# A QK-norm attention followed by a low-rank mixer MLP: two passes through DRAM against one fused pass with token rows on chip

## The chip, the cores and the metric

The kernel runs on one core of one Trainium2 chip. The metric is device time in microseconds (us), from the first to the last instruction of one execution as the device counts it; lower is better. The engines have short names in the profile: PE is the matmul engine (TensorE), PEld its weight loads, DVE is VectorE, ACT is ScalarE, POOL is GpSimd, and SP issues most of the DMAs. "L109" is line 109 of the kernel that the line comes from.

## The reference, cut to what matters

```python
# q, k, v: (8, 12, 448, 64) float32, as (batch, head, token, head_dim)
def rmsnorm(x, g):
    return x / np.sqrt(np.mean(x * x, axis=-1, keepdims=True) + 1e-06) * g
q_n, k_n = rmsnorm(q, g_q), rmsnorm(k, g_k)
scores = (1 / np.sqrt(64)) * q_n @ k_n.transpose(0, 1, 3, 2)
attn = softmax(scores)                      # over the last axis
attn_out = attn @ v
x = attn_out.transpose(0, 2, 1, 3).reshape(8, 448, 768)

# U: (448, 32), V: (32, 448), w_ch1: (768, 3072), w_ch2: (3072, 768)
h = (x.transpose(0, 2, 1) @ U @ V).transpose(0, 2, 1)     # mixes tokens, rank 32
u = x + h
out = u + np.maximum(u @ w_ch1, 0.0) @ w_ch2
```

(`softmax` stands for six lines of the reference that subtract the maximum, exponentiate and divide by the sum.)

## The kernel before

It has two stages. Attention works with the head dimension on partitions, so its result is transposed and every head's denominator is a single row on one partition. It goes to DRAM. The MLP stage first loads and casts all weights, builds the full mixing matrix `I + U V`, and then reads the attention result back.

```python
# attention, for each of 8 x 12 heads
for ki in range(NSP):                                     # NSP = 4
    sc = psum.tile([SP, S], FP32, tag="sc")               # SP = 112, S = 448
    nc.tensor.matmul(sc, knT[:, ki * SP:(ki + 1) * SP], qnT, start=True, stop=True)     # L106
    sce = work.tile([SP, S], BF16, tag="sce")
    nc.scalar.activation(sce, sc, AF.Exp, scale=scal)
    nc.tensor.matmul(avT, va_all[:, ki, h, :], sce, ...)                                # L109
den = work.tile([1, S], FP32, tag="den")
nc.vector.reciprocal(den, avT[D:D + 1, :])                                              # L111
denb = work.tile([D, S], FP32, tag="denb")
nc.gpsimd.partition_broadcast(denb, den)
oT = work.tile([D, S], BF16, tag="oT")
nc.vector.tensor_mul(oT, avT[:D, :], denb)
nc.sync.dma_start(x_scratch[b, h * D:(h + 1) * D, :], oT)
# ... cut: the norm of q and k per batch, the transposes of each head (L97)

# MLP, for each of 8 batches, after all weights are loaded and cast
# ... cut: load xT, transpose to xb, uTb = mixing with the 448 x 448 matrix (L176)
for hti in range(KH):                                     # KH = 24, KD = 6
    for dti in range(KD):
        nc.tensor.matmul(ph1, w1b[:, dti, hti * P:(hti + 1) * P], uTb[:, dti, :], ...)  # L184
    nc.scalar.activation(hT[:, hti, :], ph1, AF.Relu)
for dti in range(KD):
    for hti in range(KH):
        nc.tensor.matmul(po, w2b[:, hti, dti * P:(dti + 1) * P], hT[:, hti, :], ...)    # L192
    nc.vector.tensor_add(ofin, po, uTb[:, dti, :])
    # ... cut: transpose back to token rows, copy to osb
```

The softmax here doesn't subtract the row's maximum and nothing guards it: scores larger than these inputs give would overflow.

Of the kernel before, what the change touches and what calls it, by code (L numbers as in the profile page):

```python
# [9 lines left out]
FP32 = mybir.dt.float32  # L11
BF16 = mybir.dt.bfloat16
AX = mybir.AxisListType.X
AF = mybir.ActivationFunctionType


@with_exitstack
def kernel(
# [21 lines left out]
    SP = 112  # L40
    NSP = S // SP
    assert S == SP * NSP
    KD = dm // P
    KH = dh // P

    import dataclasses as _dc
    dram = ctx.enter_context(tc.tile_pool(name="dram", bufs=1, space=bass.MemoryType.DRAM))
    x_scratch = dram.tile([B, dm, S], BF16)
    KS = NSP

    with tc.tile_pool(name="a_const", bufs=1) as consts, \
         tc.tile_pool(name="a_norm", bufs=2) as npool, \
         tc.tile_pool(name="a_work", bufs=3) as work, \
         tc.tile_pool(name="a_ps", bufs=2, space=bass.MemoryType.PSUM) as psum, \
         tc.tile_pool(name="a_ps2", bufs=2, space=bass.MemoryType.PSUM) as psum2, \
         tc.tile_pool(name="a_ps3", bufs=2, space=bass.MemoryType.PSUM) as psum3:

        ident = consts.tile([P, P], BF16)
        make_identity(nc, ident)
        scal = 1.0 / (D ** 0.5)  # L60

        g_qs = consts.tile([D, 1], FP32)
        nc.sync.dma_start(g_qs, g_q.rearrange("(d o) -> d o", o=1))
        g_ks = consts.tile([D, 1], FP32)
        nc.sync.dma_start(g_ks, g_k.rearrange("(d o) -> d o", o=1))

        def rmsnorm_b(src, tag):
            t = npool.tile([SP, NSP, H, D], FP32, tag=tag + "_t")
            for so in range(NSP):
                nc.sync.dma_start(t[:, so, :, :], src[so * SP:(so + 1) * SP, :, :])  # L70
            sq = npool.tile([SP, NSP, H, D], FP32, tag=tag + "_sq")
            nc.scalar.activation(sq, t, AF.Square)  # L72
            ssq = npool.tile([SP, NSP, H], FP32, tag=tag + "_ssq")
            nc.vector.tensor_reduce(ssq, sq, AX, AluOpType.add)  # L74
            nc.scalar.activation(ssq, ssq, AF.Copy, scale=1.0 / D, bias=1e-6)
            nc.vector.reciprocal(ssq, ssq)
            nc.scalar.sqrt(ssq, ssq)  # L77
            ob = npool.tile([SP, NSP, H, D], BF16, tag=tag + "_ob")
            nc.vector.tensor_tensor(ob, t, ssq.rearrange("p a h -> p a h ()").to_broadcast([SP, NSP, H, D]), AluOpType.mult)  # L79
            return ob  # L80

        for b in range(B):
            qnb = rmsnorm_b(q.rearrange("b h s d -> b s h d")[b], "q")
            knb = rmsnorm_b(k.rearrange("b h s d -> b s h d")[b], "k")
            vt = npool.tile([SP, NSP, H, D], FP32, tag="vt")
            for so in range(NSP):
                nc.sync.dma_start(vt[:, so, :, :], v.rearrange("b h s d -> b s h d")[b, so * SP:(so + 1) * SP, :, :])
            va_all = npool.tile([SP, NSP, H, D + 1], BF16, tag="vaall")
            nc.gpsimd.memset(va_all[:, :, :, D:D + 1], 1.0)
            nc.vector.tensor_copy(va_all[:, :, :, :D], vt)  # L90

            for h in range(H):
                qkT = []
                for (src, gs, tg) in [(qnb, g_qs, "qT"), (knb, g_ks, "kT")]:
                    pt = psum2.tile([D, S], BF16, tag="pt")
                    for si in range(NSP):
                        nc.tensor.transpose(pt[:, si * SP:(si + 1) * SP], src[:, si, h, :], ident[:SP, :SP])  # L97
                    tT = work.tile([D, S], BF16, tag=tg)
                    nc.scalar.activation(tT, pt, AF.Copy, scale=gs)  # L99
                    qkT.append(tT)  # L100
                qnT, knT = qkT

                avT = psum3.tile([D + 1, S], FP32, tag="avT")
                for ki in range(NSP):
                    sc = psum.tile([SP, S], FP32, tag="sc")
                    nc.tensor.matmul(sc, knT[:, ki * SP:(ki + 1) * SP], qnT, start=True, stop=True)  # L106
                    sce = work.tile([SP, S], BF16, tag="sce")
                    nc.scalar.activation(sce, sc, AF.Exp, scale=scal)  # L108
                    nc.tensor.matmul(avT, va_all[:, ki, h, :], sce, start=(ki == 0), stop=(ki == NSP - 1))  # L109
                den = work.tile([1, S], FP32, tag="den")  # L110
                nc.vector.reciprocal(den, avT[D:D + 1, :])  # L111
                denb = work.tile([D, S], FP32, tag="denb")
                nc.gpsimd.partition_broadcast(denb, den)  # L113
                oT = work.tile([D, S], BF16, tag="oT")
                nc.vector.tensor_mul(oT, avT[:D, :], denb)  # L115
                nc.sync.dma_start(x_scratch[b, h * D:(h + 1) * D, :], oT)

    with tc.tile_pool(name="m_const", bufs=1) as mconsts, \
         tc.tile_pool(name="m_work", bufs=2) as work, \
         tc.tile_pool(name="m_ps", bufs=2, space=bass.MemoryType.PSUM) as psum, \  # L120
         tc.tile_pool(name="m_psout", bufs=2, space=bass.MemoryType.PSUM) as psum_out:

        identmb = mconsts.tile([P, P], BF16)
        make_identity(nc, identmb)
        w1b = mconsts.tile([P, KD, dh], BF16)
        w2b = mconsts.tile([P, KH, dm], BF16)
        Wb = mconsts.tile([SP, KS, S], BF16)
        with tc.tile_pool(name="m_tmp", bufs=1) as tmp:
            for i in range(KD):
                wf = tmp.tile([P, dh], FP32, tag="wf")  # L130
                nc.sync.dma_start(wf, moe_w_ch1.rearrange("(o i) h -> i o h", i=P)[:, i, :])
                nc.vector.tensor_copy(w1b[:, i, :], wf)  # L132
            for i in range(KH):
                wf = tmp.tile([P, dm], FP32, tag="wf")
                nc.sync.dma_start(wf, moe_w_ch2.rearrange("(o i) d -> i o d", i=P)[:, i, :])
                nc.vector.tensor_copy(w2b[:, i, :], wf)  # L136

            ident2 = tmp.tile([P, P], FP32, tag="ident2")
            make_identity(nc, ident2)
            Ub = tmp.tile([rank, S], BF16, tag="uvb")  # L140
            for si in range(KS):
                Us = tmp.tile([SP, rank], FP32, tag="us")
                nc.sync.dma_start(Us, moe_U[si * SP:(si + 1) * SP, :])
                Upt = psum.tile([rank, SP], FP32, tag="ps1")
                nc.tensor.transpose(Upt, Us, ident2[:SP, :SP])
                nc.vector.tensor_copy(Ub[:, si * SP:(si + 1) * SP], Upt)
            Vb = tmp.tile([rank, S], BF16, tag="uvb2")
            Vf = tmp.tile([rank, S], FP32, tag="uvf")
            nc.sync.dma_start(Vf, moe_V)
            nc.vector.tensor_copy(Vb, Vf)  # L150
            idstripe = tmp.tile([SP, S], FP32, tag="ids")
            for si in range(KS):
                pw = psum.tile([SP, S], FP32, tag="ps1")
                nc.tensor.matmul(pw, Ub[:, si * SP:(si + 1) * SP], Vb, start=True, stop=True)
                nc.gpsimd.memset(idstripe, 0.0)
                nc.gpsimd.affine_select(out=idstripe, in_=idstripe,
                                        compare_op=AluOpType.not_equal, fill=1.0,
                                        base=si * SP, pattern=[[-1, S]], channel_multiplier=1)
                nc.vector.tensor_add(pw, pw, idstripe)
                nc.vector.tensor_copy(Wb[:, si, :], pw)  # L160

        for b in range(B):
            xT = work.tile([P, KD, S], BF16, tag="xT")
            nc.sync.dma_start(xT, x_scratch.rearrange("b (do di) s -> b di do s", di=P)[b])
            xb = work.tile([SP, KS, dm], BF16, tag="xb")
            for dti in range(KD):
                xpt = psum.tile([SP, KS, P], BF16, tag="psx")
                for si in range(KS):
                    nc.tensor.transpose(xpt[:, si, :], xT[:, dti, si * SP:(si + 1) * SP], identmb)
                nc.vector.tensor_copy(xb[:, :, dti * P:(dti + 1) * P], xpt)  # L170

            uTb = work.tile([P, KD, S], BF16, tag="uTb")
            for dti in range(KD):
                ph = psum.tile([P, S], FP32, tag="ps1")
# [57 lines left out]
```

## Time and profile before

The time is 1167.03 us, the median of two runs (1166.46 to 1167.61). The profiled execution spans 1165.7 us.

| what | before |
|---|---|
| attention, start to last value matmul | 0 to 579 us |
| first MLP matmul (L184) | 618 us |
| PE busy | 1004.5 us, 86% |
| DVE busy | 601.6 us, of which the reciprocals 281.9 us |
| same 448 columns, distance of back-to-back matmul starts | 379 ns in attention, 189 ns in the MLP |

The first line below is the page's list of busy times, the others are from its rows of 40 slices, in which a digit is the busy share in tenths and PEclk is the clock granted to the matmul engine.

```profile
PE 1004.5 (86%) x4424; PEld 457.6 (39%) x4424; DVE 601.6 (52%) x483; ACT 495.7 (43%) x847; POOL 94.3 (8%) x122
...
PE   0888788788988899999744996999999999999997
DVE  3688989998788769667754121330212212130302
PEclk9999999999999999999996898899999999999998
```

PE looks busy nearly everywhere. The dent in slices 20 to 22 is the wait for weights between the stages. DVE is near its limit in the first half and little used in the second.

The next lines are the page's groups: line, engine, operation, output and input, shape and count, then total busy us and the mean ns of one, and after the second bar the idle time before it and what ended that.

```profile
L111 DVE RECIPROCAL den<-avT 1x448 f32<-1x448 f32 x96 | 281.9, 2944 | 80.3 <-PE avT L109 79.1
...
L109 PE MATMUL avT<-sce,va_all 112*65 112x448 bf16 x384 | 196.1, 571 | 46.4 <-ACT sce L108 43.8
L106 PE MATMUL sc<-tT 64*112 64x448 bf16 x384 | 217.1, 599 | 14.2 <-ACT sce L108 13.1
```

One reciprocal of 448 numbers on one partition takes 2.944 us. The reciprocals do not bound the stage alone: over the 579 us of attention PE is busy for 478.3 us and DVE for 460.1 us, DVE more in the first half and PE more in the second. The windows below give busy us of each engine in a stretch, then the granted clock, the DMA share and GB/s.

```profile
480.00:540.00 60.00, 57.52 (x181) 21.95 (x179) 39.86 (x23) 36.02 (x68) 8.26 (x12) 1.00 0.05 12
573.00:660.00 87.00, 48.40 (x217) 24.01 (x218) 37.81 (x55) 10.56 (x20) 7.15 (x15) 0.86 0.51 176
840.00:900.00 60.00, 60.00 (x330) 30.89 (x329) 10.40 (x17) 13.06 (x24) 0.00 (x0) 1.00 0.07 24
```

In the same 60 us PE executes 181 matmuls of attention and 330 of the MLP, and is about fully busy in both. The timeline explains that. Its columns are start, duration of the run of instructions, engine, line, operation and count.

```profile
501.77 1.81 PE L109 MATMUL avT<-sce,va_all 112*65 112x448 bf16 x4
503.51 0.62 PE L106 MATMUL sc<-tT 64*112 64x448 bf16 x1
...
859.70 1.30 PE L184 MATMUL ph_6161<-uTb,w1b 128*128 128x448 bf16 x6
```

Four matmuls of 448 columns take 1.81 us in attention, and six of 448 columns take 1.30 us in the MLP. From the start times in the trace the distances are 379 and 189 ns. The array runs attention at half clock, although the PEclk row shows nines there. The recorded clock has no change before 616.6 us, and the profile takes that for full speed.

### The profile page before, as it was taken

To read this page: it belongs to the slowest core of one execution; us is meant where nothing else is said; L and a number is where in the kernel's file an instruction comes from. 1 tells how busy PE (TensorE), PEld (TensorE's weight loads), DVE (VectorE), ACT (ScalarE), POOL (GpSimd) and SP (SyncE) were. 2 spreads that over 40 slices of the span, in tenths; PEclk is the share of its full clock that TensorE was granted. 3 is DMA by queue.
4 is the path that set the end of the run, shared out by engine and by line. 5 is a ranking of instruction groups with operands and counts; after the bars stand their busy time and mean duration, and the time that the engine had idled before them with its cause. 6 is when DMAs were issued, how large, how long until landed. Compare 5 with 4: busy or idle time off the path is not lost.

```text
span 1165.7 us, 11492 instructions
## 1 busy us (share of the span) xinstructions
PE 1004.5 (86%) x4424; PEld 457.6 (39%) x4424; DVE 601.6 (52%) x483; ACT 495.7 (43%) x847; POOL 94.3 (8%) x122
## 2 busy tenths in 40 slices
PE   0888788788988899999744996999999999999997
PEld 0333233333333333333221443455555555555553
DVE  3688989998788769667754121330212212130302
ACT  3677877777676665666400421004040312112130
POOL 0012312211111111111110000000000000000000
PEclk9999999999999999999996898899999999999998
DMA  9567766243260000000075334011010202010101
GB/s 179 96 105 129 127 117 117 53 96 58 45 120 8 13 10 12 13 12 8 12 260 191 109 109 127 18 42 41 1 48 1 71 1 71 1 48 1 48 1 48
DMA packets 153703, 74.79 MB, mean 64 GB/s; under 512 B 133904, under 2 KB 146224, under 8 KB 152880
## 3 DMA queue, kind: packets, MB, share of 16 engines
q1 hardware_dynamic: 153648, 74.06, 27.7%
q8 instruction: 34, 0.56, 0.2%
q14 instruction: 21, 0.17, 0.0%
HBM read 57.52 MB, written 16.52 MB: 64 GB/s over the span
## 4 chain that ended last, share of the span: by engine, by line
PE 69%; ACT 9%; DMA 8%; issue 7%; DVE 5%; POOL 1%; SPq 0%; POOLq 0%; ACTq 0%; DVEq 0%
PE po L192 18%; PE sc L106 13%; PE avT L109 13%; DMA wf<-in_moe_w_ch_dram 7%; PE pt L97 6%; ACT sce L108 4%; PE ph L176 3%; ACT tT L99 2%; PE ot L198 2%; DVE w2b L136 1%; ACT L77 1%; ACT L108 1%; DVE ob L79 1%; DVE den L111 1%; DVE w1b L132 1%
## 5 line engine op out<-in xcount | busy, mean ns | idle before, releaser
L111 DVE RECIPROCAL den<-avT 1x448 f32<-1x448 f32 x96 | 281.9, 2944 | 80.3 <-PE avT L109 79.1
L108 ACT ACTIVATE sce<-sc 112x448 bf16<-112x448 f32 x384 | 200.0, 542 | 158.3 <-PE sc L106 115.3
L192 PE MATMUL po<-hT,w2b 128*128 128x448 bf16 x1152 | 231.5, 356 | 13.1 <-DVE w2b L136 12.9
L109 PE MATMUL avT<-sce,va_all 112*65 112x448 bf16 x384 | 196.1, 571 | 46.4 <-ACT sce L108 43.8
L106 PE MATMUL sc<-tT 64*112 64x448 bf16 x384 | 217.1, 599 | 14.2 <-ACT sce L108 13.1
L195 DVE TENSOR_TENSOR ofin<-po,uTb 128x448 bf16<-128x448 f32 x48 | 29.9, 625 | 312.2 <-PE po L192 312.2
L184 PEld LDWEIGHTS <-w1b 128*128 128x128 bf16 x1152 | 113.3, 99 | 125.6 <-DVE w1b L132 17.5
L192 PEld LDWEIGHTS <-w2b 128*128 128x128 bf16 x1152 | 110.3, 98 | 115.7 <-DVE w2b L136 19.9
L97 PE MATMUL pt<-ident,ob 112*64 112x112 bf16 x768 | 103.4, 292 | 40.1 <-DVE ob L79 31.4
L106 PEld LDWEIGHTS <-tT 64*112 64x112 bf16 x384 | 61.2, 178 | 168.1 <-issue 160.0
L113 POOL PARTITION_BROADCAST denb<-den x96 | 86.4, 900 | 461.6 <-DVE den L111 461.5
L97 PEld LDWEIGHTS <-ob 112*64 112x64 bf16 x768 | 74.3, 159 | 121.2 <-PE sc L106 42.5
L109 PEld LDWEIGHTS <-va_all 112*65 112x65 bf16 x384 | 51.3, 146 | 102.4 <-issue 85.1
L115 DVE TENSOR_TENSOR oT<-avT,denb 64x448 bf16<-64x448 f32 x96 | 59.2, 617 | 18.2 <-POOL denb L113 16.8
L99 ACT ACTIVATE tT<-pt,g_ks 64x448 bf16<-64x448 bf16 x96 | 59.7, 622 | 8.0 <-PE pt L97 4.3
L74 DVE TENSOR_REDUCE ssq<-sq 112x48 f32<-112x3072 f32 x16 | 53.0, 3311 | 19.1 <-ACT sq L72 19.1
L99 ACT ACTIVATE tT<-pt,g_qs 64x448 bf16<-64x448 bf16 x96 | 59.5, 620 | 3.0 <-PE pt L97 1.9
L79 DVE TENSOR_TENSOR ob<-t,ssq 112x3072 bf16<-112x3072 f32 x16 | 53.2, 3325 | 1.4 <-ACT ssq L77 1.4
L136 DVE CAST w2b<-wf 128x768 bf16<-128x768 f32 x24 | 13.4, 560 | 65.6 <-DMA wf<-in_moe_w_ch_dram 65.6
L176 PE MATMUL ph<-Wb,xb 112*128 112x448 bf16 x192 | 44.2, 368 | 1.2 <-DVE uTb L178 0.6
L72 ACT ACTIVATE sq<-t 112x3072 f32<-112x3072 f32 x16 | 44.1, 2754 | 0.0
L199 DVE CAST osb<-ot 112x512 f32<-112x512 bf16 x48 | 33.1, 690 | 21.1 <-PE ot L198 21.1
(420 smaller groups left out, 599.4 us busy)
## 6 DMA issues: line engine op xcount, KB each, us to landing
t<-in_q_dram SPq DMA_DIRECT2D x32, 336.0 KB, 5.1
t<-in_k_dram SPq DMA_DIRECT2D x32, 336.0 KB, 5.3
vt<-in_v_dram SPq DMA_DIRECT2D x32, 336.0 KB, 5.8
out_dram<-osb SPq DMA_DIRECT2D x32, 336.0 KB, 4.2
wf<-in_moe_w_ch_dram SPq DMA_DIRECT2D x6, 1536.0 KB, 6.7
wf<-in_moe_w_ch_dram SPq DMA_DIRECT2D x24, 384.0 KB, 3.0
x_scratch<-oT SPq DMA_DIRECT2D x96, 56.0 KB, 1.9
xT<-x_scratch SPq DMA_DIRECT2D x8, 672.0 KB, 4.8
```

The lines of the kernel that those rows point to most:

```text
L79: nc.vector.tensor_tensor(ob, t, ssq.rearrange("p a h -> p a h ()").to_broadcast([SP, NSP, H, D]), AluOpType.mult)
L97: nc.tensor.transpose(pt[:, si * SP:(si + 1) * SP], src[:, si, h, :], ident[:SP, :SP])
L99: nc.scalar.activation(tT, pt, AF.Copy, scale=gs)
L106: nc.tensor.matmul(sc, knT[:, ki * SP:(ki + 1) * SP], qnT, start=True, stop=True)
L108: nc.scalar.activation(sce, sc, AF.Exp, scale=scal)
L109: nc.tensor.matmul(avT, va_all[:, ki, h, :], sce, start=(ki == 0), stop=(ki == NSP - 1))
L111: nc.vector.reciprocal(den, avT[D:D + 1, :])
L113: nc.gpsimd.partition_broadcast(denb, den)
L115: nc.vector.tensor_mul(oT, avT[:D, :], denb)
L176: nc.tensor.matmul(ph, xb[:, si, dti * P:(dti + 1) * P], Wb[:, si, :], start=(si == 0), stop=(si == KS - 1))
L184: nc.tensor.matmul(ph1, w1b[:, dti, hti * P:(hti + 1) * P], uTb[:, dti, :], start=(dti == 0), stop=(dti == KD - 1))
L192: nc.tensor.matmul(po, w2b[:, hti, dti * P:(dti + 1) * P], hT[:, hti, :], start=(hti == 0), stop=(hti == KH - 1))
```

## The change

The intent is one pass. A token of a batch is taken as `4 p + j`, so that one DMA row holds four tokens. The value product is turned around, so that the exponentials are the stationary operand and tokens land on partitions. Denominators then sit one to a partition, and the division is a small reciprocal of 128 x 4 and a multiply. Attention output stays in SBUF. Mixing is two small products of rank 32. The second MLP product makes `hT` stationary, so token rows come out and need no transpose. Weights are cast by their DMA. The squares and the inverse root of the norm move to POOL. The instructions of the next batch's attention are written ahead of this batch's MLP, and a scheduler interleaves them in each engine's fixed order. The core of the diff, with cuts:

```diff
-            nc.scalar.activation(sq, t, AF.Square)
-            nc.vector.tensor_reduce(ssq, sq, AX, AluOpType.add)
-            nc.scalar.activation(ssq, ssq, AF.Copy, scale=1.0 / D, bias=1e-6)
-            nc.vector.reciprocal(ssq, ssq)
-            nc.scalar.sqrt(ssq, ssq)
+            for s in range(2):
+                nc.gpsimd.tensor_tensor(sq[:, s], qk[:, s], qk[:, s], OP.mult)           # L150
+            nc.vector.tensor_reduce(rstd..., sq..., AX, OP.add)                          # L152
+            nc.gpsimd.tensor_scalar(rstd, rstd, D * 1e-6, None, OP.add)                  # L154
+            nc.gpsimd.tensor_tensor(rs, rs, mhalf, OP.pow)                               # L156
...
+                    nc.vector.tensor_tensor(qkn..., qk..., rstd..., OP.mult)             # L163
...
-                    nc.tensor.matmul(avT, va_all[:, ki, h, :], sce, ...)
-                nc.vector.reciprocal(den, avT[D:D + 1, :])
-                nc.gpsimd.partition_broadcast(denb, den)
-                nc.vector.tensor_mul(oT, avT[:D, :], denb)
-                nc.sync.dma_start(x_scratch[b, h * D:(h + 1) * D, :], oT)
+                    o = ps_o.tile([P, 4, D + 1], FP32, tag="o")            # one buffer
+                    for i, off in enumerate(OFFS[par]):
+                        for kc in range(NJ):
+                            nc.tensor.matmul(o[:, i, :], E[:, hh, c:c + P], va[:, hl, kc, :], ...)  # L193
+                    nc.vector.reciprocal(rec, o[:, :, D])                                # L196
+                    nc.vector.tensor_tensor(x3[:, :, d0:d0 + D], o..., rec..., OP.mult)  # L197
+                    nc.vector.tensor_tensor(xs[rows, d0:d0 + D], o..., rec..., OP.mult)  # L200
...
-                for hti in range(KH):
-                    nc.tensor.matmul(po, w2b[:, hti, dti * P:(dti + 1) * P], hT[:, hti, :], ...)
-                for si in range(KS):
-                    nc.tensor.transpose(ot[:, si, :], ofin[:, si * SP:(si + 1) * SP], identmb)
+                for hc in range(KH):
+                    nc.tensor.matmul(po, hT[:, hc, i * P:(i + 1) * P], w2b[:, hc, hs], ...)  # L270
...
+    attention(0)
+    load_weights(state["gate"])
+    setup_mix()
+    mix(0)
+    attention(1)
+    mlp(0)
+    for b in range(1, B):
+        mix(b)                                   # L217 to L236
+        if b + 1 < B:
+            attention(b + 1)
+        mlp(b)                                   # w1: L250, w2: L270
```

## The prediction

> **What bounds the kernel now.** The 1165.7 us span has two stages that hardly overlap. Until about 575 us it is attention. There, by the busy-time windows, PE is 48 to 57 busy of 60 us, DVE 40 to 56. The MLP runs from 600 us; from 780 us PE is 60 of 60. Between them, 573 to 660 us and again 713 to 735 us, PE waits for weights (the chain of waits: issue 18.4 us, `wf` loads 4 to 7 us each).
>
> The distance between matmul starts tells more than busy time. In the MLP, 448 columns start 189 ns apart. In attention, back-to-back `avT` matmuls of the same 448 columns start 379 ns apart, `sc` 415 ns, transposes 93 ns against 48 to 56. The clock row shows full speed there; I distrust it: attention runs at half clock. The Trainium skill, "TensorE: Matmul & The Clock Gate", Part 1, says low activity halves the clock; the trace agrees by spacing. Attention's matmuls fill under half of the array (64x112, 112x65). The recorded drops at 623 and 719 us follow about 30% array use; 66% kept full clock.
>
> **Removed.** The 2.94 us reciprocals on one partition (282 us of DVE), the broadcasts, the DRAM round trip, 30 table loads (38 us of ACT), both transposes around the MLP, the weight bubble (about 100 us).
>
> **PE after, per batch, warm (estimates from the spacings).** MLP columns are unchanged: w1 144 at 189 = 27.2 us, w2 168 at about 163 = 27.3, V products 1.3. Transposes 48 at 50 = 2.4. Scores 48 in row halves, 5 to 10. Values: 192 pairs of a 128-column load and 65 moving columns, 30 to 60 ns each, 6 to 11. Mixing 3.5. Sum 73 to 83 us, over eight batches 585 to 665.
>
> **DVE after, per batch**, at about 1.04 ns per element plus 150 ns: reduce 6.7, qkn 8.0, q/k copies 4.7, per-head normalisation 9.3, mixing 5.3, relus 7.5, adds 3.9 = 45 us. ACT: 24 exps of 896 columns at about 0.92 us, plus relus = 28. POOL about 25, with `pow` unmeasured.
>
> **Critical path.** The instruction order gives, per batch, an attention stretch (next batch's attention with about half of w1) and a dense tail (other half of w1, then w2; 41 us). The stretch holds about 37 us of PE and 38 us of DVE; with one `o` bank, one `t` bank and a fixed order I expect 42 to 50 us. So 86 us a batch. Startup, attention 0 alone (cold) and attention 1 beside mlp 0, with 19 MB of weights arriving: mlp 0 ends near 150 us. Then 6 x 86 + 63 (last batch, no attention) gives about **735 us**, range 665 to 860. Faster by over 2%: 0.97; within 2%: 0.02; slower: 0.01.
>
> **Right if:** 384-column `po` start about 163 ns apart; w1 matmuls inside the attention stretch keep 163 to 216 ns (warm); DVE about 360 us in total, no reciprocal group above 25 us; PE has no gap above 10 us after about 130 us; the tail is about 41 us, the stretch 42 to 50.
>
> **Wrong if:** the stretch falls back to half clock: w1 there at about 375 ns, +30 us a batch, 900 us. Or POOL's `pow`, or its descriptor writing for the casting weight loads, takes many microseconds and starves attention at the start; or the fixed order stalls PE on DVE's chain after each head.

## The result and the profile after

The time is 857.29 us, the median of two runs (855.32 to 859.25). Ratios here are the mean time of one kernel's fast runs over that of the other's of the same rounds, so not quite the ratio of the quoted medians: 0.734, with a 95% interval of 0.7318 to 0.7363. The time fell by 310 us where 432 were predicted. It is inside the range that was given, but at its upper edge (860). All outputs are right.

First the page of the profile after, its busy times and its row of slices:

```profile
PE 688.1 (80%) x5168; PEld 383.7 (45%) x5168; DVE 373.7 (44%) x749; ACT 215.4 (25%) x289; POOL 274.9 (32%) x162
...
PE   0365576898679976798679976799868998998997
POOL 5885676301760016700661005630275000000000
PEclk9995587799899996899989999789969999999999
```

DVE fell to 373.7 us, near the 360 predicted. PE is no longer full: it dips once in each batch, and the granted clock dips with it. POOL works in bursts at the same places. Where POOL has no more bursts, from slice 32 on, the dips are gone.

The groups show the terms that were costed and one that was not:

```profile
L270 PE MATMUL po<-w2b,hT 128*128 128x384 bf16 x1344 | 227.5, 326 | 0.0
L150 POOL TENSOR_TENSOR sq<-qk 112x1024 f32<-112x1024 f32 x48 | 95.9, 2011 | 289.8 <-DMA qk<-in_q_dram 288.3
...
L156 POOL TENSOR_TENSOR rstd<-rstd,mhalf 112x32 f32<-112x32 f32 x24 | 131.1, 5460 | 1.7
L163 DVE TENSOR_TENSOR qkn<-qk,rstd 112x512 bf16<-112x512 f32 x96 | 98.0, 1041 | 54.5 <-POOL rstd L156 54.1
```

The `pow` takes 5.46 us for 32 numbers on each partition, 24 times. That is 131.1 us of POOL's 274.9. The multiply that waits for it, `qkn`, takes 1041 ns in the mean, where 0.665 us was assumed (8.0 us a batch, twelve of them).

The list of waits says who stands behind whom: the engine and line that waited, what it waited for, total us, times, longest us.

```profile
DVE qkn L163 <- POOL rstd L156: 54.1, 10, 13.9
...
DVE rstd L152 <- POOL sq L150: 39.2, 12, 6.4
PE o L193 <- DVE xs_103 L200: 38.2, 12, 7.3
PE o L193 <- DVE xs_104 L200: 32.6, 13, 5.4
```

DVE waits for POOL, and PE's value product waits for DVE to empty the one `o` buffer. Three timelines of the same ten microseconds show how one leads to the other (a bracket gives the idle time before and what ended it). First DVE's:

```profile
326.84 0.17 DVE L196 RECIPROCAL rec<-o 128x4 f32<-128x4 f32 x1
331.13 2.37 DVE L163 TENSOR_TENSOR qkn<-qk,rstd 112x512 bf16<-112x512 f32 x1 [4.12 <-POOL rstd L156]
333.43 0.34 DVE L197 TENSOR_TENSOR x_2592<-o,rec 128x192 bf16<-128x192 f32 x1
333.79 0.23 DVE L200 TENSOR_TENSOR xs_104<-o,rec 64x64 bf16<-64x64 f32 x1
```

POOL's timeline over the same time:

```profile
325.64 5.46 POOL L156 TENSOR_TENSOR rstd<-rstd,mhalf 112x32 f32<-112x32 f32 x1
331.07 1.89 POOL L150 TENSOR_TENSOR sq<-qk 112x1024 f32<-112x1024 f32 x1
```

And PE's:

```profile
329.30 0.62 PE L182 MATMUL sc<-qT,kT 64*112 64x448 bf16 x1
334.16 1.04 PE L193 MATMUL o<-va_101,E_98 112*128 112x65 bf16 x16 [4.25 <-DVE xs_104 L200]
```

The reciprocal at 326.84 belongs to the attention that is being computed, and the two normalising multiplies (L197, L200) needed only its result. But the first `qkn` of the batch after that one stands between them in DVE's order, and it waits for the `pow`. So DVE is idle for 4.12 us with ready work behind the wait. PE stands at the value product of the next head for 4.25 us, with ready w1 matmuls behind it.

The `qkn` at 331.13 also took 2.37 us, and it ran beside POOL's squares. The longest of all took 4.14 us (61.91 to 66.05), while POOL squared from 61.44 to 65.51; the median is 0.68 us. The Trainium skill, "SBUF — State Buffer", section "Who interferes with whom", states that a DVE instruction with two SBUF inputs contends with a GpSimd instruction that reads SBUF, and that the later one blocks. The times agree: all 30 `qkn` of more than 0.8 us started while POOL was busy, and 28 of them ended 0.54 to 0.56 us after the end of the square or the cast of v that POOL was running at their start.

The windows below are three whole batches, from the start of one mixing to that of the next:

```profile
502.40:597.10 94.70, 76.76 (x625) 45.13 (x625) 46.31 (x95) 25.83 (x36) 32.80 (x15) 0.91 0.22 57
597.10:704.40 107.30, 93.74 (x674) 49.32 (x674) 45.80 (x91) 27.43 (x36) 32.35 (x15) 0.92 0.18 45
704.40:780.90 76.50, 71.02 (x621) 43.12 (x620) 33.27 (x88) 25.78 (x36) 0.00 (x0) 1.00 0.06 17
```

The third holds a whole attention too, that of the last batch, but no norm for a batch after it. It executes about as many matmuls as the first, at full clock, and is 18.2 us shorter. So the scheduler puts the norm of batch b+2 into the attention of batch b+1, and the batch pays for it.

With the start times of the trace, each batch splits at its last value matmul. Up to there is what the prediction called the stretch, and the rest is its tail:

| mixing starts at us | stretch | tail | sum |
|---|---|---|---|
| 192.8 | 58.0 | 48.5 | 106.5 |
| 299.3 | 61.5 | 33.9 | 95.4 |
| 394.7 | 59.2 | 48.5 | 107.7 |
| 502.4 | 60.7 | 34.0 | 94.7 |
| 597.1 | 58.8 | 48.5 | 107.3 |
| mean of five | 59.6 | 42.7 | 102.3 |
| 704.4 (no norm inside) | 36.4 | 40.1 | 76.5 |
| predicted | 42 to 50 | 41 | 86 |

(Tails alternate because a batch's w2 covers three or four tiles of tokens.)

### The profile page after: what moved, and what is told of

Same layout as the page of the kernel before. It is cut to its first block, busy times and chain, and to the rows that moved or that the text cites. A ratio compares the mean times of both kernels' runs of the same rounds, so it can differ in the third digit from the quotient of the medians.

```text
span 857.2 us, 12102 instructions
## 1 busy us (share of the span) xinstructions
PE 688.1 (80%) x5168; PEld 383.7 (45%) x5168; DVE 373.7 (44%) x749; ACT 215.4 (25%) x289; POOL 274.9 (32%) x162
## 4 chain that ended last, share of the span: by engine, by line
PE 53%; DVE 22%; POOL 18%; DMA 4%; issue 2%; ACT 1%; ACTq 0%; SPq 0%; POOLq 0%
PE po L270 25%; PE ph L250 19%; POOL rstd L156 10%; DVE qkn L163 8%; DVE rstd L152 6%; POOL sq L150 6%; PE o L193 3%; DMA qk<-in_q_dram 2%; DVE uB L236 2%; PE pu L227 2%; DVE uA L233 1%; PE sc L182 1%; PE pu L230 1%; DMA vt<-in_v_dram 1%; DVE qT L175 1%
## 5 line engine op out<-in xcount | busy, mean ns | idle before, releaser
L270 PE MATMUL po<-w2b,hT 128*128 128x384 bf16 x1344 | 227.5, 326 | 0.0
L150 POOL TENSOR_TENSOR sq<-qk 112x1024 f32<-112x1024 f32 x48 | 95.9, 2011 | 289.8 <-DMA qk<-in_q_dram 288.3
L270 PEld LDWEIGHTS <-hT 128*128 128x128 bf16 x1344 | 131.5, 98 | 86.9
L253 ACT ACTIVATE hT<-ph 128x384 bf16<-128x384 f32 (+1 forms) x96 | 52.3, 545 | 460.3 <-PE ph L250 460.1
L250 PE MATMUL ph<-uB,w1b 128*128 128x512 bf16 x576 | 146.5, 396 | 2.2 <-ACT hT L253 1.9
L250 PE MATMUL ph<-uA,w1b 128*128 128x384 bf16 x576 | 126.8, 357 | 16.2 <-DVE uA L233 14.3
L156 POOL TENSOR_TENSOR rstd<-rstd,mhalf 112x32 f32<-112x32 f32 x24 | 131.1, 5460 | 1.7
L163 DVE TENSOR_TENSOR qkn<-qk,rstd 112x512 bf16<-112x512 f32 x96 | 98.0, 1041 | 54.5 <-POOL rstd L156 54.1
L184 ACT ACTIVATE E_99<-sc 112x896 bf16<-112x896 f32 x96 | 83.4, 917 | 57.9 <-PE sc L182 43.1
L184 ACT ACTIVATE E_98<-sc 112x896 bf16<-112x896 f32 x96 | 83.2, 917 | 57.0 <-PE sc L182 31.6
L182 PE MATMUL sc<-qT,kT 64*112 64x448 bf16 x384 | 83.2, 433 | 8.7 <-DVE kT L176 3.3
L193 PEld LDWEIGHTS <-E_98 112*128 112x128 bf16 x768 | 36.5, 110 | 83.5 <-issue 42.7
L171 PEld LDWEIGHTS <-qkn 112*128 112x128 bf16 x384 | 23.4, 105 | 60.2 <-DVE qkn L163 43.9
L193 PEld LDWEIGHTS <-E_99 112*128 112x128 bf16 x768 | 33.8, 107 | 20.2 <-issue 10.2
L193 PE MATMUL o<-va_102,E_98 112*128 112x65 bf16 x256 | 13.7, 216 | 29.7 <-DVE xs_103 L200 16.4
L196 DVE RECIPROCAL rec<-o 128x4 f32<-128x4 f32 x96 | 17.1, 178 | 40.1 <-PE o L193 39.9
```

The costliest lines, as they stand in the source:

```text
L150: nc.gpsimd.tensor_tensor(sq[:, s], qk[:, s], qk[:, s], OP.mult)
L156: nc.gpsimd.tensor_tensor(rs, rs, mhalf, OP.pow)
L163: nc.vector.tensor_tensor(qkn[:, s].rearrange("p j h d -> p h j d"), qk[:, s, hp].rearrange("p h (j d) -> p h j d", d=D), rstd[:, s, hp].r ...
L171: nc.tensor.transpose(pt[:, s, j * SP:(j + 1) * SP], qkn[:, s, j].rearrange("p h d -> p (h d)"), ident[:SP, :SP])
L182: nc.tensor.matmul(sc[:, hh, 0:S], kT[pp, kc * SP:(kc + 1) * SP], qT[pp, :], start=True, stop=True)
L184: nc.scalar.activation(E[:, :, PAD + kc * S:PAD + (kc + 1) * S], sc[:, :, 0:S], AF.Exp, scale=float(D) ** 0.5)
```

## The experiments

Theory A: the norm on POOL is what holds the stretch, through DVE's and PE's fixed orders. Theory B: q and k come too late, because two load buffers are too few (POOL's squares waited 288.3 us for them in the list of waits). Theory C: one `o` and one `t` bank hold the stretch whatever the norm costs. Every ratio is to the kernel before, whose median in the three jobs was 1164.83, 1164.35 and 1166.05 us.

| run | what it is | us (runs) | ratio |
|---|---|---|---|
| after | the change | 857.29 (2) | 0.734 |
| e1_rsqrt_dve | inverse root on DVE | 787.97 (4) | 0.6763 |
| e2_loads3 | third load buffer | 856.77 (4) | 0.7352 |
| e3_sq_act | squares on ACT | 781.29 (4) | 0.6704 |
| e5_pow2 | `pow` twice | 948.81 (4) | 0.8163 |
| e4_rsqrt_sq | e1 and e3 | 749.26 (4) | 0.6426 |
| e7_o2t2 | two `o`, two `t` banks | 836.32 (4) | 0.7185 |
| e10_rsqrt_sq_o2t2 | e4 and e7 | 744.45 (4) | 0.6396 |
| e9_rsqrt_sq_pu | e4, mixing product in the MLP's banks | 721.04 (4) | 0.6179 |
| e13_rsqrt_sq_pu_s3o2 | e9 with other score banks | 743.56 (4) | 0.6364 |
| e8_barrier | the change, stages kept apart | 1085.76 (4) | 0.9327 |
| e11_rsqrt_sq_barrier | e4, stages kept apart | 916.05 (4) | 0.7851 |
| e12_before_warm | before, with dummy matmuls | 1276.07 (2) | 1.0928 |

### The inverse root on DVE, the squares on ACT, and the `pow` doubled

e1 takes `add` and `pow` from POOL and computes the inverse root on DVE, from a shifted start value and two Newton steps. It leaves out the epsilon; the output still matched.

```diff
-            nc.gpsimd.tensor_scalar(rstd, rstd, D * 1e-6, None, OP.add)
-            nc.gpsimd.tensor_tensor(rs, rs, mhalf, OP.pow)
+            nc.vector.tensor_scalar(t.bitcast(I32), rs.bitcast(I32), 1, None, OP.logical_shift_right)
+            nc.vector.tensor_scalar(y.bitcast(I32), t.bitcast(I32), -1, 0x5f3759df, OP.mult, OP.add)
+            for it in range(2):
+                nc.vector.scalar_tensor_tensor(t, y, -0.5, y, OP.mult, OP.mult)
+                nc.vector.tensor_tensor(t, t, rs, OP.mult)
+                nc.vector.scalar_tensor_tensor(rs if it else y, t, 1.5, y, OP.add, OP.mult)
```

> Edit: the POOL add and pow (5.46 us each) are replaced by eight small DVE operations (bit-shift seed and two Newton steps) that directly follow the reduce on the same queue. Theory A (the in-order DVE queue holds the next batch's qkn, which waits for pow, ahead of this batch's per-head work, and PE waits for that through the one o bank): qkn waits on POOL rstd (54 us) vanish, part of the reduce waits (39 us) and of the half-clock time with them; about 785 us, 760 to 815. Rival B (the loads are late because only two load buffers exist, so POOL starts late, and the length of pow is secondary): within 2% of 857. Rival C (one o bank and one t bank stall PE whatever the norm does): within 2% of 857.

Measured: 787.97 us (785.83 to 789.81), against an expected 785. (Of the two POOL operations taken away, the `pow` is the one of 5.46 us; the `add` took 0.30 us.) The eight new instructions cost DVE 52.9 us in all, and yet the kernel is 69 us faster. B and C both fall as the main cause, for neither lets this edit gain anything.

e3 leaves `pow` where it is and moves the squares to ACT (1071 ns each there).

```diff
-                nc.gpsimd.tensor_tensor(sq[:, s], qk[:, s], qk[:, s], OP.mult)
+                nc.scalar.activation(sq[:, s], qk[:, s], AF.Square)
```

> Edit: the squares go from POOL (2.0 us each) to ACT as Square activations; pow stays on POOL. Theory A plus [...]contention (qkn takes 0.68 us alone and up to 4.1 us while POOL squares): qkn mean falls from 1.04 to about 0.70 us, the chain before each reduce is 2 us shorter, about 820 us (795 to 845). Rival B and C: within 2% of 857.

Measured: 781.29 us, 76 us less than the change, which is more than was expected. The list of waits of e3:

```profile
DVE qkn L163 <- POOL rstd L156: 37.1, 10, 5.7
...
PE o L193 <- DVE xs L200: 30.6, 13, 6.8
```

DVE's wait for the `pow` fell from 54.1 to 37.1 us, and the wait of PE's value product from 70.8 to 30.6 us. `qkn` fell from 1041 to 717 ns in the mean, 98 to 66.7 us in all: with no squares on POOL, little is left to block it. Theory A alone had left that part out. The edit also makes the squares themselves shorter (1.07 us on ACT, 2.01 us on POOL) and frees POOL of them; which of these parts brings how much of the 76 us was not separated.

e5 computes the `pow` a second time, into a tile that nobody reads, before the real one.

```diff
+            rs2 = norm.tile([SP, 2 * HG * NJ], FP32, tag="rs2")
+            nc.gpsimd.tensor_tensor(rs2, rs, mhalf, OP.pow)
             nc.gpsimd.tensor_tensor(rs, rs, mhalf, OP.pow)
```

> Edit: every pow is done twice on POOL, the first into a spare tile; results unchanged. If pow sits on the critical chain (theory A) most of the 24 extra pows of 5.46 us (131 us) show: 930 to 985 us. If it is hidden (B, C): less than 20 us more, 857 to 877.

Measured: 948.81 us (947.74 to 958.62), 91.5 us more. The added work is another 131 us of POOL, so 70% of it shows in the time. In the list of waits of e5 PE's value product now waits more than twice as long:

```profile
PE o L195 <- DVE xs L202: 153.1, 26, 11.1
DVE rstd L152 <- POOL sq L150: 103.5, 15, 15.8
...
DVE qkn L165 <- POOL rstd L158: 77.4, 12, 9.7
```

POOL, busy for only 32% of the change's span, is thus on the critical path.

### Both at once

e4 holds the edits of e1 and of e3 together.

> Edit: both earlier edits together, reciprocal root on DVE and squares on ACT; POOL keeps only the v cast and the weight loads. Theory A: the two shorten one chain at different places (pow 5.5 us; squares 4 us and the slowed qkn), so the savings of 69 and 76 us should mostly add: 735 us, 710 to 760, DVE waits for the norm (qkn on POOL rstd, reduce on sq) under 20 us in sum, half clock after the first full-clock stretch under 50 us. If both only removed the same wait: 770 to 785.

Measured: 749.26 us (742.3 to 752.75), against an expected 735. Windows of e4, for the batches from 407.6 to 664.3 us:

```profile
407.60:492.00 84.40, 76.73 (x625) 44.58 (x625) 46.41 (x119) 31.09 (x42) 3.67 (x3) 0.92 0.24 64
492.00:587.80 95.80, 87.33 (x667) 47.71 (x676) 46.53 (x115) 32.52 (x42) 3.24 (x3) 1.00 0.20 51
587.80:664.30 76.50, 71.05 (x625) 43.10 (x625) 33.22 (x88) 25.74 (x36) 0.00 (x0) 1.00 0.06 17
```

With POOL out of the norm, the five steady batches take 93.8, 80.0, 94.5, 84.4 and 95.8 us, 89.7 in the mean. Their stretches, by the start times in the trace, are 41.1, 43.9, 40.9, 48.2 and 46.2 us, where the prediction had 42 to 50. mlp 0 ends at 139 us instead of 193. No start-to-start gap of PE after 130 us is longer than 1.6 us, where the change had gaps up to 7.6. In e4's list of waits PE's value product waits for DVE for 7.2 us, where the change had 70.8. The page's chain of the work that ended last, by engine, says the same. In the change it is:

```profile
PE 53%; DVE 22%; POOL 18%; DMA 4%; issue 2%; ACT 1%; ACTq 0%; SPq 0%; POOLq 0%
```

And in e4, where POOL is no longer in it:

```profile
PE 61%; DVE 19%; DMA 10%; ACT 6%; issue 3%; ACTq 0%; SPq 0%
```

### More load buffers

```diff
-    opool = ctx.enter_context(tc.tile_pool(name="opool", bufs=3))
+    opool = ctx.enter_context(tc.tile_pool(name="opool", bufs=2))
-            qk = loads.tile([SP, 2, HG, NJ * D], FP32, tag="qk")
+            qk = loads.tile([SP, 2, HG, NJ * D], FP32, tag="qk", bufs=3)
-            rstd = norm.tile([SP, 2, HG, NJ], FP32, tag="rstd")
+            rstd = norm.tile([SP, 2, HG, NJ], FP32, tag="rstd", bufs=3)
```

> Edit: three qk buffers and three rstd buffers in place of two, paid for with two osb buffers in place of three; pow stays on POOL. Theory A: helps only where pow thereby moves into the dense tail; 820 us, 790 to 850. Rival B: POOL works in the tail, the stretch falls from 71-75 us to near the 52 us of the last one; about 765 us. Rival C: within 2% of 857.

Measured: 856.77 us (853.11 to 859.4), no difference. POOL's squares still wait 283.0 us for `qk`. Loads are released by the `qkn` of an earlier group, inside the stretch, and a third buffer only shifts that by one group. So this miss is of the edit: it does not test loads that arrive early in the tail, and that question stays open. It does show that more buffers alone buy nothing in the sum: the five steady batches take 98.6 us in the mean instead of 102.3, but mlp 0 ends at 205 us instead of 193. The run also narrows theory A. In these five batches DVE's `qkn` no longer waited for the `pow` (20.7 us in the change), but its reduce waited 46.9 us for POOL's squares instead of 28.1. So it is POOL's whole chain of the norm that holds the stretch, not only the wait at the `pow`.

### More banks

```diff
-    ps_s = ctx.enter_context(tc.tile_pool(name="ps_s", bufs=2, space=bass.MemoryType.PSUM))
-    ps_o = ctx.enter_context(tc.tile_pool(name="ps_o", bufs=1, space=bass.MemoryType.PSUM))
-    ps_t = ctx.enter_context(tc.tile_pool(name="ps_t", bufs=1, space=bass.MemoryType.PSUM))
+    ps_s = ctx.enter_context(tc.tile_pool(name="ps_s", bufs=1, space=bass.MemoryType.PSUM))
+    ps_o = ctx.enter_context(tc.tile_pool(name="ps_o", bufs=2, space=bass.MemoryType.PSUM))
+    ps_t = ctx.enter_context(tc.tile_pool(name="ps_t", bufs=2, space=bass.MemoryType.PSUM))
```

> Edit: PSUM only, of the changed kernel: two o banks and two t banks, paid for with one score tile of two banks in place of two. Rival C (the single o and t banks hold PE): 857 falls by over 5%, to about 800. Theory A (PE waits for DVE, which waits for the norm; another o bank only delays that by one head, and one score tile exposes exp): 840 to 890.

Measured: 836.32 us, 2.4% faster than the change, and just under what theory A gave (840 to 890). C has a small part. The same edit on e4:

> Edit: reciprocal root on DVE and squares on ACT, plus the two o and two t banks with one score tile. Once DVE no longer waits for the norm, what is left of PE's waits is for the o and t banks: if those count, 20 to 40 us under e4_rsqrt_sq; if the single score tile costs as much (PE then waits for exp, 0.92 us, before each score pair), within 10 us of it or slower.

Measured: 744.45 us against 749.26, no clear difference, since e4's own runs spread from 742.3 to 752.75. The steady batches got shorter (91.2, 76.3, 90.5, 75.6 and 90.2 us), but the start got longer: mlp 0 ends at 172 us instead of 139. With the single score tile PE's score products waited 34.6 us for exponentials in the first 170 us, where e4 has 9.1 us of that wait in its whole span. So the banks are needed in more than one place. Moving one tile to a pool that has room at that moment does better:

```diff
-            pu = ps_t.tile([P, S], FP32, tag="t")
+            pu = ps_mm.tile([P, S], FP32, tag="mm")
```

> Edit: e4_rsqrt_sq with the mixing product pu in the two mm banks in place of the single t bank. In the mixing PE waits 0.65 us for each of six evacuations per batch; two banks should hide most of it: 720 to 742 us. If the w1 filler that used the mm banks there is only pushed back: within 1% of 749.

Measured: 721.04 us (720.2 to 723.61), the best version of all. It is 0.6179 of the time before, and 136 us under the change. Its row of slices:

```profile
PE   0685699999899999999899998998999999999997
PEclk9996899999999999999999999999999999999999
```

The dips are gone; what is left is the start. Stretches are now 39.9, 39.6, 38.6, 39.1 and 38.3 us. In the last try, three score banks of one head each and two `o` banks were put on top:

```diff
-    ps_s = ctx.enter_context(tc.tile_pool(name="ps_s", bufs=2, space=bass.MemoryType.PSUM))
-    ps_o = ctx.enter_context(tc.tile_pool(name="ps_o", bufs=1, space=bass.MemoryType.PSUM))
+    ps_s = ctx.enter_context(tc.tile_pool(name="ps_s", bufs=3, space=bass.MemoryType.PSUM))
+    ps_o = ctx.enter_context(tc.tile_pool(name="ps_o", bufs=2, space=bass.MemoryType.PSUM))
-                    sc = ps_s.tile([SP, 2, 512], FP32, tag="s")
+                    scs = [ps_s.tile([SP, 512], FP32, tag="s", name=f"sc{hh}") for hh in range(2)]
```

(The matmuls and the exponentials follow: one of each per head.)

> Edit: e9_rsqrt_sq_pu with one score bank per head (three of them) in place of two pairs, exp of 448 columns in place of 896, and two o banks from the bank set free. PE no longer waits for xs between heads: 700 to 735 us. If the doubled number of exps (26 in place of 22 us a batch) or the score banks hold PE instead: 740 or more.

Measured: 743.56 us, slower than e9. The edit also doubled the number of exponentials, and which of its parts costs the 22 us was not separated.

### What the overlap is worth

Barriers of all engines keep mixing, attention and MLP apart; nothing else differs from the change.

```diff
         mix(b)
         if b + 1 < B:
+            tc.strict_bb_all_engine_barrier()
             attention(b + 1)
+            tc.strict_bb_all_engine_barrier()
         mlp(b)
```

(A third barrier stands between `attention(1)` and `mlp(0)`.)

> Edit: the changed kernel with an all-engine barrier before and after each attention from the second on, so that attention and MLP of one batch no longer overlap; all instructions stay. If the overlap carries a part of the gain: mixing 10, attention 45 to 55, MLP 62 us in turn, 960 to 1060 us, attention at half clock again (w1 not in it). If the gain comes from removed work alone: 840 to 900.

Measured: 1085.76 us, above the 960 to 1060 expected, 229 us more than the change and 7% under before. The same barriers on e4:

> Edit: e4_rsqrt_sq with the barriers of e8_barrier. It asks how much of the 229 us that the barriers cost was overlap of attention with the MLP and how much was the norm chain laid bare. If overlap (and the clock that w1 keeps up): still over 150 us slower than e4_rsqrt_sq, 900 to 960. If it was mostly the norm chain: under 850.

Measured: 916.05 us, 167 us more than e4. So with the norm off POOL, the removed work and shorter stages alone take before's time down by 250 us, and interleaving takes another 167. That is not PE's overlap alone: the barriers also hold back the loads and the norm of the next batch, and PE's transposes wait 93.4 us for `qkn` in e11, against 16.1 in e4. In the change interleaving also hid part of the POOL chain, which is the likely reason for the difference of 62 us between the two figures (229 and 167). A part of both figures is the clock: after the first return to full clock, the trace's clock records add up to 476 us at half clock in e8 and 322 in e11, against 151 in the change and 41 in e4.

### The clock in the kernel before

If attention ran at half clock because it uses too little of the array, added dummy matmuls should raise the clock and bring the known full-clock distances.

```diff
                     nc.tensor.matmul(avT, va_all[:, ki, h, :], sce, ...)
+                    for _ in range(4):
+                        nc.tensor.matmul(dum, wdum[:SP, :], sce, start=True, stop=True)
```

> Edit: the kernel before, with four extra 112x128 by 448 matmuls per score tile into a spare bank that nobody reads: 1536 more matmuls, array use in attention from about 30% to over 70%. If array use sets the clock: after the first head or two avT, transposes and the rest run at full clock (448 columns 189 ns apart in back-to-back dummies, transposes 48 to 56 ns), so the 3 us of added work per head hide in PE's freed time and the total stays within about 4% of 1165. If the half clock has another cause: the dummies run 379 ns apart and attention grows by over 300 us, to 1450 or more.

Measured: the mechanism as expected, the time not. The timeline of PE in e12:

```profile
502.25 0.92 PE L115 MATMUL dum<-sce,wdum 112*128 112x448 bf16 x4
...
504.55 0.58 PE L101 MATMUL pt<-ident,ob 112*64 112x112 bf16 x8
```

Eight transposes take 0.58 us, where before eight took 1.05 us (at 500.06 us there). The dummies start 188 to 189 ns apart, transposes 48 to 50 ns, and score matmuls 233 ns instead of 415. Attention runs at full clock for most of its length from 39.6 us on. So before's attention was at half clock, and more work in the array was enough to end that. The dummies raise two things at once, the filled area and the time in which columns stream; the last section has what the traces say on which of them counts.

The time rose to 1276.07 us because the dummies stand in PE's order. 1536 of them at about 189 ns are 290 us of PE, and the last value matmul came at 687 us instead of 579, 108 us later. An estimate from these numbers: at full clock PE's own work in the stage takes some 180 us less. The stage could not have become shorter by that much, for DVE is busy for 460.1 of its 579 us, which leaves at most 119. Dummy matmuls cannot collect that gain; filling the array with useful matmuls, as the interleaving does, can.

## Why the prediction was right or wrong

**What bounds the kernel before: right.** Two stages with a weight wait between them, and attention at half clock in spite of the clock row. e12 shows the last by experiment. The Trainium skill, "TensorE: Matmul & The Clock Gate", Part 1, describes the half rate and the return to full rate; the distances of 379 and 189 ns agree.

**What is removed and the column costs: right.** `po` matmuls of 384 columns start 162 ns apart (163 predicted), w1 matmuls 161 to 163 and 215 to 216 ns apart when warm (163 to 216; in the cold parts of the stretch about 320 and 427), DVE is 373.7 us (360), and the largest reciprocal group is 17.1 us (under 25). No weight wait of PE is left in the list of waits, and no idle time of PE after 130 us exceeds 10 us (the longest is 7.3).

**The tail: right.** It is 42.7 us in the mean of five batches, 41 predicted.

**The step that failed** is: "The stretch holds about 37 us of PE and 38 us of DVE; with one `o` bank, one `t` bank and a fixed order I expect 42 to 50 us. So 86 us a batch." The stretch measured 59.6 us, and a batch 102.3. The sum of loads of PE and DVE was the wrong thing to sum: POOL was put at "about 25, with `pow` unmeasured" and taken to be beside the path. It was 34 us a batch (274.9 over 8), of which `pow` 16.4 us, and it stood in series with DVE, which stood in series with PE. This was on the prediction's own list of what would make it wrong: POOL's `pow`, and PE stalled by the fixed order on DVE's chain.

The two runs e1 and e5 show it from both sides: without `pow`, 69 us less; with two, 91.5 us more. e4 shows that the rest of the step was nearly sound: with the norm off POOL the stretches are 41 to 48 us and the kernel takes 749 us, where 735 was predicted.

That the time still lies in the range is luck of a wide range: it reached to 860, and the sum missed by 122 us. The miss adds up, in us against the predicted sum of 150 + 6 x 86 + 63 = 729:

| term | predicted | measured | miss |
|---|---|---|---|
| until mlp 0 ends | 150 | 192.8 | +43 |
| five steady batches | 430 | 511.6 | +82 |
| the batch with attention 7 | 86 | 76.5 | -10 |
| the last batch | 63 | 71.3 | +8 |
| stores after the last w2, and rounding | 6 | 5.0 | -1 |
| sum | 735 | 857.2 | +122 |

Both large terms lie where POOL does the norm. In e4 the first is 139 us, under the prediction, and the five batches 448.5 us, 18.5 over it.

Two smaller sizes were off. `qkn` was put at 8.0 us a batch and took 12.3 us (98.0 over 8), through the contention with POOL's squares. And the stretch was partly cold. After the first return to full clock at 53.4 us, the trace's records show 150.7 us at half clock, 16 stretches in all, against 41.0 in e4. At half clock the array does half as much, so of the 108 us between the two kernels at most about (150.7 - 41.0) / 2 = 55 us can be the clock, and less where PE only waited. (If the start too ran at half clock, 53.4 us in the change and 29.2 in e4, that adds at most 12 us.) The clock is a consequence here: the edits that took POOL's work away did not touch PE, and the half-clock time fell. The fallback that the prediction named ("+30 us a batch") came only in part.

Two things stay open: whether loads that arrive early would hide the POOL chain without moving it, since e2 did not bring that about, and how the 62 us between e8 and e11 split up.

## What to carry to other kernels

Before a cheap-looking elementwise operation moves to an engine that seems idle, measure that one operation: taking the norm off the engine at 32% busy saved 108 us here, because two in-order queues stood in line behind it. When a scheduler interleaves two batches, cost the longest chain through the engines, and look for instructions of the next batch that wait ahead of ready work of this one. And read the matmul clock from distances of equal matmuls, not from the clock row or from busy time alone.

## What the Trainium skill lacked or had wrong

- "GPSIMD Engine Reference", section 3.1, has elementwise costs but none for `pow`. Here `pow` took 5.46 us for 112 x 32 numbers, about 171 ns for each of the 32, while a multiply of 112 x 1024 took 2.01 us.
- "TensorE: Matmul & The Clock Gate", Part 1, ties full clock to about 3.4 us of being busy. Attention before was busy for 57.52 of 60 us and stayed at half clock to the end. The use of the array was reckoned for windows of 3.41 us (the step of the clock records): the time in which columns stream, at the measured 189 ns for 448 columns or twice that, weighted by the rows and columns filled. In before's attention it was at most 0.39. In the 14 traces here the first full clock came after windows at 0.72 to 0.89, and no earlier window was above 0.70. Without the weights the two overlap: up to 0.86 without effect, and 0.81 with it. So filled area is the reading that fits better. The page has no such threshold, and these runs do not fix one: later windows at up to 0.77 were not followed by full clock, and some at 0.65 were.
- The same part warns that clock records can be unreliable. A concrete form is missing: before the first recorded change, at 616.6 us here, the profile shows full clock where 379 ns for 448 columns says half.
- "TensorEngine Tiling (Array Packing)", Key Properties, says that a change of tiling mode drains the engine, but gives no cost. Here the start after a change between the row-half scores and other matmuls came 278 to 326 ns after a score matmul of 448 columns, which alone would account for 189 ns (the distance of 448 columns in before's MLP); the change cost the rest, some 90 to 137 ns.
